# Two quarters of the last inverse step in one two-bank PSUM buffer

## The chip, the core and the metric

The kernel runs on one core of a Trainium2 chip. Its engines each work through a queue of their own in order: TensorE (PE in the profile) multiplies matrices into PSUM, ScalarE (ACT) and VectorE (DVE) read PSUM and write SBUF, GpSimd (POOL) works on SBUF alone, and SyncE (SP) issues nearly all transfers. PSUM has eight banks of 512 fp32 numbers on each of 128 partitions. The metric is the device time of one execution in microseconds (us), lower is better.

## What is computed

A gate per position mixes two branches of the same input `u` (2048 positions, 640 channels): a long convolution (S4D) and a dense layer with ReLU.

```python
K = 2.0 * jnp.einsum("dn,dnl->dl", C, P).real           # kernel of 2048 taps per channel
y = jnp.fft.irfft(rfft(u, 2L) * rfft(K, 2L), 2L)[:L]     # long convolution
a = y + u * D_skip
b = jnp.maximum(x @ w1, 0) @ w2                          # 640 -> 1728 -> 640
g = sigmoid((x * gate_w).sum(-1))
return g * a + (1 - g) * b
```

## The kernel before

The 640 channels of the convolution are done in five tiles of 128 (called tile 0 to tile 4 here, `i` in the code). In each tile the transforms are small matrix multiplications on PE, with their results in PSUM tiles named `pc`, from a pool of three buffers of two banks each (the ring `psc`):

- stage 1 (constants `tf`): the transform along one index of the taps (tiles `ck`, `cl`) and of the input (`xu`); VectorE transposes the results into the tile `ku`.
- stage 2 (`tm`): eight products for a tile, each 16 matmuls into one `pc` buffer. ScalarE copies one bank (`COPY ku<-pc`, 512 columns), VectorE multiplies with the other (two `TENSOR_TENSOR ku<-pc,ku`), GpSimd adds and subtracts. The buffer comes free after the second multiplication.
- inverse step 2 (`tn`): two halves of 64 matmuls, two `pc` buffers each, copied back by ScalarE; then eight transposes on VectorE (`STREAM_TRANSPOSE ku<-ku`), the relays.
- inverse step 1 (`tw`, function `inv1`): the last step. It is cut in four quarters per tile, a pair for each of `j = 0, 1`. A quarter is two matmuls of 512 columns, one for each half of the partitions, that fill one bank. ScalarE then scales it with the gate in four instructions (`ACTIVATE yo<-pc,gate`). Before, each quarter takes a whole `pc` buffer of two banks and leaves the second bank empty.

The dense layer runs beside this. Its 128-wide products write the other two banks (tiles `pf`) and fill PE between the steps of the convolution. It is done in three passes over parts of the hidden width; sums of a pass are loaded (`q<-part`), scaled on ScalarE (`ACTIVATE q<-q,omg`), added to on VectorE (`q<-pf,omg,q`) and stored (`part<-q`, `out_dram<-q`). A `q` load waits for stores of the same rows, and on SP's queue it stands behind other transfers, the loads `yj<-part` among them. Finished convolution rows leave through `yo`: stored to a scratch tensor `y_`, or added to the dense rows and stored to the output.

The order is not written by hand. Every group of instructions is a task with a duration, dependencies, a priority and the ring slots that it takes and uses. `Plan.run` (line 222) simulates the five engines with these numbers when the program is built and calls the tasks in that order; the recorded order of each engine is then kept. A buffer token goes back to its ring when all the tasks that take or use it are through. So a change of who takes a slot changes the order of everything behind it. The planner's rings, and the order that comes from them, set no wait by themselves: the waits that the program holds are derived from the tiles that its instructions read and write.

Of the kernel before, what the change touches and what calls it, by code (L numbers as in the profile page):

```python
# [10 lines left out]
F32 = mybir.dt.float32  # L11
# [14 lines left out]
S4R = 3  # L26
# [318 lines left out]
class Kernel:  # L345
# [865 lines left out]
    def conv(self, C=128):  # L1211
        tc, nc, io, A, tok, ring = self.tc, self.nc, self.io, self.plan.add, self.plan.token, self.plan.ring
# [6 lines left out]
        st = {}  # L1219
# [8 lines left out]
        def table(k, shape, src):  # L1228
            def go():
                st[k] = self.pr.tile(shape, F32, name=k)  # L1230
                D_.dma_start(st[k], io[src])
            return A('SP', 'tab', 0.62, go, [opened], kb=math.prod(shape) * 4 / 1024, rank=3)
# [34 lines left out]
        K, first, pes = {}, {}, {}  # L1267
# [126 lines left out]
        def inv1(i, j, dep):  # L1394
            last = i == n - 1
            for q in range(2):
                b_, b0 = tok('psc'), j * 8 + q * 4
                ns = min(max(2 * sum(c <= i for c in CG) - b0, 0), 4)
                y_ = tok('yo') if ns or not last else None
                g_, first = None, False  # L1400
                if last and ns < 4:
                    first = self.gy_tok is None
                    g_ = self.gy_tok = self.gy_tok or tok('K')

                def pe(q=q, b0=b0):
                    py = st['p4', i, b0] = self.psc.tile([128, 2, 4, C], F32, name="pc")
                    for h in range(2):
                        self.E.matmul(py[h * 64:h * 64 + 64, 0].rearrange("p b c -> p (b c)"), st['tw'],
                                      st['K', i][:, h * 4 + b0 // 4], start=True, stop=True)

                def copy(q=q, b0=b0, ns=ns, y_=y_, first=first):
                    if first:
                        self.gy = self.pr.tile([128, 8, 2, 512], F32, name="ku", bufs=2).rearrange("p j k (b c) -> p (j k b) c", c=C)
                    if y_:
                        st['yo', i, b0] = self.pr.tile([128, 4, C], F32, name="yo", bufs=YO)
                    x = st['p4', i, b0][:, 0].rearrange("p b c -> p (b c)").rearrange("p (c b) -> p b c", b=4)
                    for b in range(4):
                        o = self.gy[:, b0 + b] if last and b >= ns else st['yo', i, b0][:, b]
                        S.mul(o, x[:, b], self.gate[:, b0 + b:b0 + b + 1])
                a = A('PE', 's4', 0.87, pe, [*dep, tw], take=[b_], use=[K[i]], rank=S4R, mode='c1')  # L1420
                pes['4', i, b0] = a
                if JS4 and q:
                    self.plan.join([pes['4', i, b0 - 4], a])
                c = A('ACT', 's4', 1.24, copy, [a], take=[x for x in (y_, g_ if first else None) if x],
                      use=[b_] + ([g_] if g_ and not first else []), rank=S4A)
                self.need_gates.append(c)
                if ns < 4:
                    if not last:
                        def store(b0=b0, ns=ns):
                            stq.dma_start(self.sc['y'][:, b0 + ns:b0 + 4, i * C:i * C + C], st['yo', i, b0][:, ns:])  # L1430
                        c2 = A(STQ, 'y4', 0.62, store, [c], use=[y_], kb=64 * (4 - ns), rank=STR, late=True)
                    self.y_st[i, b0 // 4] = c if last else c2
                if ns:

                    new = not last or b0 == 0
                    if last:
                        j_ = self.yl_tok = tok('cu') if new else self.yl_tok
                    else:
                        j_ = tok('yj')

                    def load(b0=b0, ns=ns):
                        if last:
                            if b0 == 0:
                                st['yl'] = self.xu[:, :16 * C].rearrange(
                                    "p (b c) -> p b c", c=C)
                            st['yj', i, b0] = st['yl'][:, b0:b0 + 4]
                        else:
                            st['yj', i, b0] = self.pr.tile([128, 4, C], F32, name="yj", bufs=YJ)
                        for b in range(0, ns, 2):
                            D_.dma_start(st['yj', i, b0][:, b:b + 2],  # L1450
                                         self.sc['part'][(len(PARTS) - 1) % 2][(b0 + b) // 2][:, :, i * C:i * C + C])

                    def join(b0=b0, ns=ns):
                        y = st['yo', i, b0][:, :ns]
                        P.tensor_add(y, y, st['yj', i, b0][:, :ns])

                    def out(b0=b0, ns=ns):
                        for h in range(2):
                            stq.dma_start(od[h, :, b0:b0 + ns, i * C:i * C + C], st['yo', i, b0][64 * h:64 * h + 64, :ns])
                    ld = A('SP', 'yq', 0.62 * ((ns + 1) // 2), load, [opened], take=[j_] if new else (), use=() if new else [j_],  # L1460
                           kb=64 * ns, rank=3)
                    self.need_sums.append((ld, [(b0 + b) // 2 for b in range(0, ns, 2)]))
                    own = A('POOL', 's4', 0.1 + 0.3 * ns, join, [c, ld], use=[y_, j_], rank=2)
                    A(STQ, 'y4', 1.25, out, [own], use=[y_], kb=64 * ns, rank=STR, late=True)
# [6 lines left out]
        tm, tw, tn = table('tm', [128, 32, 64], 't_m'), table('tw', [128, 64], 't_w'), table('tn', [128, 8, 2, 2, 64], 't_n')  # L1471
        lk.update({q: load_k(0, q) for q in range(2, 4)})
        dep = [x for q in range(4) for x in stage1('k', 0, q, lk[q])]
        dep += [x for q in range(4) for x in stage1('u', 0, q, u)]
        for i in range(n):
            more = i + 1 < n
            if more:
                u = load_u(i + 1)
            fs = [stage2(i, j, [*dep, tm]) for j in range(8)]
            iv = [inv2(i, h, [x for j in range(4 * h, 4 * h + 4) for x in fs[j][1]]) for h in range(2)]  # L1480
            for j in range(8):
                self.plan.put(fs[j][0], 's2')
                if JS2 and j % 2:
                    self.plan.join([fs[j - 1][0], fs[j][0]])
                if j == 3 + LATE:
                    [self.plan.put(x, 's2') for x in iv[0][0]]
            [self.plan.put(x, 's2') for x in iv[1][0]]
            xs, new = [x for _, y in iv for x in y], []
            if more:
                for q in range(4):  # L1490
                    new += stage1('k', i + 1, q, load_k(i + 1, q))
            rl = [relay(i, r, xs) for r in range(8)]
            if more:
                for q in range(4):
                    new += stage1('u', i + 1, q, u)
            for j in range(2):
                inv1(i, j, rl)
            dep = new
# [42 lines left out]
```

## Time and profile before

| | us |
|---|---|
| median of 3 runs | 644.57 (643.60 to 645.45) |
| the profiled execution | 642.35 |
| its span in the profile | 640.6 |

| engine | busy, us | share of the span |
|---|---|---|
| PE (matmul) | 617.3 | 96% |
| DVE | 508.5 | 79% |
| ACT | 402.1 | 63% |
| POOL | 93.9 | 15% |

The convolution's part of the span begins at about 407 us and the first `tw` at 478 us. The granted PE clock is at full speed in every slice. In the timeline a row is a run of equal instructions: start, length, engine, operation, count; in brackets the idle time before it and what ended it. An fp32 matmul (`tf`, `tm`, `tn`, `tw`) leaves two records, so a quarter of `tw` shows as x4 and a product of `tm` as x32; the `pf` matmuls leave one each. Since matmul ends are modelled, a wait of PE is read best from start to start. Nearly all rows carry line 314, that of a helper which records every operation, so one goes by the tiles' names.

### The profile page before, as it was taken

What the parts mean: (1) busy time and instruction counts of PE and PEld (TensorE: products, weight loads), DVE (VectorE), ACT (ScalarE), POOL (GpSimd) and SP (SyncE); (2) the same over time, 40 slices, a digit from 0 to 9 for tenths busy, and PEclk for the clock granted to TensorE, in tenths of its full rate; (3) what the DMA queues carried; (4) which work ended last, traced back from release to release, by engine and by line L of the source; (5) the groups of instructions that cost most, each with busy time, mean ns of one, the idle gap of its engine ahead of it and who ended that gap; (6) DMA issues with size and microseconds to landing.
All of it is one profiled execution on the core that took longest, in us unless ns stands there. A gap on an engine that the chain in (4) does not pass through costs nothing.

```text
span 640.6 us, 19212 instructions
## 1 busy us (share of the span) xinstructions
PE 617.3 (96%) x8236; PEld 503.0 (79%) x8236; DVE 508.5 (79%) x818; ACT 402.1 (63%) x603; POOL 93.9 (15%) x134
## 2 busy tenths in 40 slices
PE   7989999899999899999999999999999999999897
PEld 6989998798898798898898898665565556756577
DVE  4889936989999999998999999768579753966542
ACT  5557439999999988988978985113443424432550
POOL 0000000000000000000000000024151531713633
PEclk9999999999999999999999999999999999999999
DMA  9974774333456734373454225794406558156355
GB/s 256 326 236 147 221 229 165 105 125 112 136 167 210 255 122 144 122 242 117 129 198 154 79 80 176 258 315 132 144 3 215 185 164 263 53 158 188 102 166 133
DMA packets 76176, 107.78 MB, mean 168 GB/s; under 512 B 7610, under 2 KB 58682, under 8 KB 75195
## 3 DMA queue, kind: packets, MB, share of 16 engines
q1 hardware_dynamic: 75930, 106.14, 53.2%
q8 instruction: 65, 1.06, 0.7%
q10 hardware_dynamic: 160, 0.41, 0.3%
q14 instruction: 21, 0.16, 0.1%
HBM read 67.47 MB, written 44.30 MB: 174 GB/s over the span
## 4 chain that ended last, share of the span: by engine, by line
PE 56%; DVE 5%; DMA 2%; ACT 2%; issue 1%; SPq 1%; DVEq 0%; ACTq 0%
PE pf L314 35%; PE pc L314 13%; PE pk L314 4%; DVE ku L314 3%; PE pg L314 2%; PE px L314 2%; DMA part<-q 1%; ACT ku L314 1%; PE pe L314 1%; DMA out_dram<-yo 1%; SPq L314 1%; DVE sn L314 1%; ACT cs L314 0%; DVE q L314 0%; ACT q L314 0%
## 5 line engine op out<-in xcount | busy, mean ns | idle before, releaser
L314 PE MATMUL pf<-xx,w1h 128*128 128x256 f32 (+1 forms) x760 | 184.2, 339 | 0.4 <-DVE xx L314 0.3
L314 PEld LDWEIGHTS pf<-xx,w1h 128*128 128x128 f32 x760 | 125.2, 189 | 22.8 <-issue 7.3
L314 PE MATMUL pf<-xx,w1l 128*128 128x512 f32 (+1 forms) x340 | 115.7, 340 | 0.0
L314 PE MATMUL pf<-w2h,hh 128*128 128x320 f32 x288 | 89.7, 315 | 2.4 <-DVE hl L314 1.5
L314 PE MATMUL pf<-w2l,hh 128*128 128x320 f32 x288 | 87.8, 309 | 0.0
L314 ACT COPY ku<-pc 128x512 f32<-128x512 f32 (+1 forms) x60 | 43.8, 761 | 68.2 <-PE pc L314 56.7
L314 PE MATMUL pf<-w2h,hl 128*128 128x320 f32 x256 | 73.3, 312 | 0.0
L314 PEld LDWEIGHTS pf<-xx,w1l 128*128 128x128 f32 x340 | 64.3, 189 | 7.6 <-DVE w1l L314 0.2
L314 POOL TENSOR_TENSOR kt<-kt,dsk 128x8 f32<-128x8 f32 x20 | 10.3, 515 | 392.7 <-DVE kt L314 377.8
L314 POOL TENSOR_TENSOR ku<-ku 128x256 f32<-128x256 f32 x80 | 56.2, 737 | 55.3 <-DVE ku L314 49.1
L314 DVE TENSOR_TENSOR ku<-pc,ku 128x512 f32<-128x512 f32 x80 | 52.6, 684 | 12.5 <-ACT ku L314 11.3
L314 DVE STREAM_TRANSPOSE ku<-pc 128x512 f32<-128x512 f32 x80 | 50.2, 683 | 13.7 <-PE pc L314 13.7
L314 PEld LDWEIGHTS pf<-w2h,hh 128*128 128x128 f32 x288 | 54.1, 188 | 7.7 <-issue 3.7
L314 DVE TENSOR_TENSOR sn<-pg,cs 128x1024 f32<-128x1024 f32 x40 | 48.7, 1217 | 7.5 <-ACT cs L314 7.5
L314 PEld LDWEIGHTS pf<-w2l,hh 128*128 128x128 f32 x288 | 54.1, 188 | 0.6
L314 ACT ACT_TABLE_LOAD x42 | 53.9, 1283 | 0.7
L314 ACT CAST cs<-pg 128x1024 int32<-128x1024 f32 x40 | 40.3, 1008 | 21.2 <-PE pg L314 21.0
L314 DVE TENSOR_TENSOR mg<-mg,cs 128x1024 f32<-128x1024 f32 x40 | 48.9, 1222 | 1.3
L314 PEld LDWEIGHTS pf<-w2h,hl 128*128 128x128 f32 x256 | 46.4, 188 | 3.5 <-issue 2.9
L314 PE MATMUL pc<-ku,tm 64*32 64x256 f32 x1280 | 42.2, 392 | 3.6 <-DVE ku L314 2.4
L314 ACT ACTIVATE cs<-cs,half_pi 128x1024 f32<-128x1024 f32 x40 | 45.6, 1140 | 0.0
L314 ACT ACTIVATE hh<-pf 128x512 fp32r<-128x512 f32 (+1 forms) x40 | 20.5, 513 | 39.4 <-PE pf L314 39.4
(170 smaller groups left out, 1232.5 us busy)
## 6 DMA issues: line engine op xcount, KB each, us to landing
xx<-xt SPq DMA_DIRECT2D x24, 640.0 KB, 6.8
xt<-xx SPq DMA_DIRECT2D x16, 640.0 KB, 3.9
part<-q SPq DMA_DIRECT2D x16, 640.0 KB, 3.4
q<-part SPq DMA_DIRECT2D x16, 640.0 KB, 5.3
ws<-in_B_w_dram SPq DMA_DIRECT2D x20, 320.0 KB, 5.5
kd<-kt SPq DMA_DIRECT2D x80, 64.0 KB, 1.8
ub<-in_A_u_dram SPq DMA_DIRECT2D x10, 512.0 KB, 4.7
xu<-ub SPq DMA_DIRECT2D x5, 1024.0 KB, 6.2
```

What stands on the lines that cost most here:

```text
L314: self._last = self._tc.keep_in_program_order(f(*a, **k))
```

## The change

The token and the tile are taken once for a pair. The first quarter (`q == 0`) takes the token and makes the tile, and writes bank 0; the second quarter uses the same token and tile and writes bank 1. The copies read the bank of their quarter. The token is free again after the copies of both quarters.

```diff
             for q in range(2):
-                b_, b0 = tok('psc'), j * 8 + q * 4
+                b0 = j * 8 + q * 4
+                b_ = b_ if q else tok('psc')
...
-                def pe(q=q, b0=b0):
-                    py = st['p4', i, b0] = self.psc.tile([128, 2, 4, C], F32, name="pc")
+                def pe(q=q, b0=b0, j=j):
+                    if not q:
+                        st['p4', i, j] = self.psc.tile([128, 2, 4, C], F32, name="pc")
+                    py = st['p4', i, j]
                     for h in range(2):
-                        self.E.matmul(py[h * 64:h * 64 + 64, 0].rearrange("p b c -> p (b c)"), st['tw'],
+                        self.E.matmul(py[h * 64:h * 64 + 64, q].rearrange("p b c -> p (b c)"), st['tw'],
                                       st['K', i][:, h * 4 + b0 // 4], start=True, stop=True)
...
-                    x = st['p4', i, b0][:, 0].rearrange("p b c -> p (b c)").rearrange("p (c b) -> p b c", b=4)
+                    x = st['p4', i, j][:, q].rearrange("p b c -> p (b c)").rearrange("p (c b) -> p b c", b=4)
...
-                a = A('PE', 's4', 0.87, pe, [*dep, tw], take=[b_], use=[K[i]], rank=S4R, mode='c1')
+                a = A('PE', 's4', 0.87, pe, [*dep, tw], take=() if q else [b_], use=[K[i]] + ([b_] if q else []), rank=S4R, mode='c1')
```

No instruction is added or taken away on any engine; PE has 5466 in both programs. What changes is the order from the first `tw` on, on all five engines, and the waits. Three places follow.

PE in tile 1, from the last `cl` product of stage 1 on (`pc` results; `pf` rows are the dense layer), before:

```order
L314 MATMUL pc<-cl,tf 64x512 x4
L314 MATMUL pc<-ku,tw 64x512 x4
L314 MATMUL pc<-ku,tm 32x256 x48
L314 MATMUL pf<-w2l_5336,w2h_6512 128x320
L314 MATMUL pf<-w2h_5335,w2l_6513 128x320
L314 MATMUL pf<-w2h_5272,hh_6024 128x320
```

and now:

```order
L314 MATMUL pc<-cl,tf 64x512 x4
L314 MATMUL pc<-ku,tw 64x512 x6
L314 MATMUL pc<-ku,tm 32x256 x32
L314 MATMUL pc<-ku,tw 64x512 x2
L314 MATMUL pc<-ku,tm 32x256 x32
L314 MATMUL pf<-w2l_5336,w2h_6530 128x320
```

Before, two quarters came first and the other two after all eight `tm` products; now all four come at the front, the last of them between the second and the third product.

PE in tile 3, the same place, with the engines whose semaphores each instruction waits for, before:

```order
L314 MATMUL pc<-ku,tw 64x512 [waits DVE_49,PE_49]
L314 MATMUL pc<-ku,tw 64x512
L314 MATMUL pc<-ku,tw 64x512 [waits DVE_49,PE_49]
L314 MATMUL pc<-ku,tw 64x512
L314 MATMUL pc<-ku,tm 32x256 [waits DVE_49,PE_49]
L314 MATMUL pc<-ku,tm 32x256 x15
L314 MATMUL pc<-ku,tm 32x256 [waits PE_49,Activation_49]
L314 MATMUL pc<-ku,tm 32x256 x15
L314 MATMUL pc<-ku,tm 32x256 [waits PE_49,Activation_49]
L314 MATMUL pc<-ku,tm 32x256 x15
```

and now:

```order
L314 MATMUL pc<-ku,tw 64x512 x3
L314 MATMUL pc<-ku,tw 64x512 [waits DVE_49,PE_49]
L314 MATMUL pc<-ku,tw 64x512
L314 MATMUL pc<-ku,tm 32x256 [waits DVE_49,PE_49]
L314 MATMUL pc<-ku,tm 32x256 x15
L314 MATMUL pc<-ku,tm 32x256 [waits PE_49,Activation_49]
L314 MATMUL pc<-ku,tm 32x256 x15
L314 MATMUL pc<-ku,tw 64x512 [waits Activation_49]
L314 MATMUL pc<-ku,tw 64x512
```

The second `tm` product now waits for ScalarE's copies of both quarters of the first pair, and the second quarter of the second pair waits for ScalarE too: the copy of the first quarter, from the other bank of the same tile, stands ahead of it in the program.

ScalarE from tile 3's first `tm` copies to tile 4's dense activations (`COPY ku<-pc 128x512` are the `tm` copies, `128x4x128x2` those of `tn`, `hh` and `w1h` hold activations of the dense layer), before:

```order
L314 COPY ku<-pc 128x512 x3
L314 ACTIVATE q<-q,omg 128x640
L314 COPY ku<-pc 128x512
L314 ACTIVATE q<-q,omg 128x640
L314 COPY ku<-pc 128x512 x4
L314 ACTIVATE yo<-pc,gate 128x128 x8
L314 COPY ku<-pc 128x4x128x2 x2
L314 ACTIVATE hh_8137<-pf 128x512
L314 COPY ku<-pc 128x4x128x2 x2
L314 ACTIVATE hh_8235<-pf 128x512
L314 ACTIVATE q<-q,omg 128x640
L314 ACTIVATE w1h_8256<-pf 128x512
```

and now:

```order
L314 COPY ku<-pc 128x512 x4
L314 ACTIVATE q<-q,omg 128x640
L314 ACTIVATE yo<-pc,gate 128x128 x4
L314 ACTIVATE q<-q,omg 128x640
L314 COPY ku<-pc 128x512 x4
L314 COPY ku<-pc 128x4x128x2 x2
L314 ACTIVATE hh_8126<-pf 128x512
L314 COPY ku<-pc 128x4x128x2 x2
L314 ACTIVATE hh_8225<-pf 128x512
L314 ACTIVATE q<-q,omg 128x640 x2
L314 ACTIVATE w1h_8251<-pf 128x512
```

The first `q` stands one `tm` copy later, the last quarter's copy stands between the two `q`, and later both `q` stand ahead of `w1h` where one stood behind it.

More of the change, by code (lines that the diff above doesn't have):

```diff
@@ L1403, in inv1, with copy @@
                     g_ = self.gy_tok = self.gy_tok or tok('K')
-                def pe(q=q, b0=b0):
-                    py = st['p4', i, b0] = self.psc.tile([128, 2, 4, C], F32, name="pc")
+                def pe(q=q, b0=b0, j=j):
+                    if not q:
+                        st['p4', i, j] = self.psc.tile([128, 2, 4, C], F32, name="pc")
+                    py = st['p4', i, j]
                     for h in range(2):
-                        self.E.matmul(py[h * 64:h * 64 + 64, 0].rearrange("p b c -> p (b c)"), st['tw'],
+                        self.E.matmul(py[h * 64:h * 64 + 64, q].rearrange("p b c -> p (b c)"), st['tw'],
                                       st['K', i][:, h * 4 + b0 // 4], start=True, stop=True)
-                def copy(q=q, b0=b0, ns=ns, y_=y_, first=first):
+                def copy(q=q, b0=b0, ns=ns, y_=y_, first=first, j=j):
                     if first:
```

## The prediction

> **What bounds the kernel now.** I read the page's first part, then the busy time by stretches of 20 us, then PE's timeline and waits where PE is not full, and last the chain that released it.
>
> ```profile
> span 640.6 us, 19212 instructions
> PE 617.3 (96%) x8236; PEld 503.0 (79%) x8236; DVE 508.5 (79%) x818; ACT 402.1 (63%) x603; POOL 93.9 (15%) x134
> ...
> 560.00:580.00 20.00, 19.86 (x251) 10.70 (x250) 14.70 (x26) 6.31 (x18) 3.56 (x3) 1.00 0.59 179
> 580.00:600.00 20.00, 17.40 (x306) 10.28 (x304) 13.61 (x23) 9.13 (x22) 13.00 (x17) 1.00 0.48 135
> 600.00:620.00 20.00, 19.96 (x328) 16.30 (x327) 7.74 (x14) 8.82 (x15) 3.96 (x6) 1.00 0.57 163
> ```
>
> PE is the bound, at a granted clock of 1.00. The change leaves its work as it is, so the time can move only by what PE waits. Between the first `tw` (478 us) and the end, one stretch has a visible hole, 580 to 600 us with 2.6 us idle: tile 3, where the first of the two `tw` pairs and the `tm` products are. PE's timeline there, and its waits from 560 to 604 us:
>
> ```profile
> 478.47 3.28 PE L314 MATMUL pc<-ku,tw 128*64 128x512 f32 x12
> ...
> 581.32 1.94 PE L314 MATMUL pc<-ku,tw 128*64 128x512 f32 x8
> 583.19 2.98 PE L314 MATMUL pc<-ku,tm 64*32 64x256 f32 x96
> 587.82 0.31 PE L314 MATMUL pf<-w2h,w2h 128*128 128x320 f32 x1
> 588.06 3.01 PE L314 MATMUL pc<-ku,tm 64*32 64x256 f32 x96
> 592.72 0.31 PE L314 MATMUL pf<-w2h,w2h 128*128 128x320 f32 x1
> 594.72 1.15 PE L314 MATMUL pc<-ku,tm 64*32 64x256 f32 x32 [1.70 <-DVE ku L314]
> 596.37 1.16 PE L314 MATMUL pc<-ku,tm 64*32 64x256 f32 x32 [0.50 <-DVE ku L314]
> 597.70 1.08 PE L314 MATMUL pc<-ku,tw 128*64 128x512 f32 x4 [0.17 <-DVE ku L314]
> 599.02 1.08 PE L314 MATMUL pc<-ku,tw 128*64 128x512 f32 x4 [0.24 <-DVE ku L314]
> ...
> PE pc L314 <- DVE ku L314: 2.6, 4, 1.7
> ```
>
> Prices from these rows: a quarter of `tw` is 1.87/2 = 0.93 us of PE (581.32 to 583.19, x8 being two quarters), a `tm` product 2.92/3 = 0.97. From start to start, with 0.2 for the step from `pf` to `pc` (588.06 - 587.82), the four waits are 594.72 - 592.72 - 0.2 = 1.8, then 0.7, 0.2 and 0.4 (each start less the one before, less the group's own 1.0 to 1.15 or 0.93): 3.0 us. The chain of waits says whose they are:
>
> ```profile
> 574.45 0.53 DVE q L314
> ...
> 576.53 6.80 DMA part<-q
> ...
> 587.53 4.29 DMA out_dram<-yo
> 591.83 0.83 ACT q L314
> 592.66 0.48 ACT ku L314
> ...
> 593.16 0.70 DVE ku L314
> ```
>
> A store of dense sums (`part<-q`) lands at 583.33, then SP issues five `yj` loads and the load of `q`; ScalarE waits for it until 591.83 (the profile names the landing of a store issued right behind the load), and behind that waiting instruction stand the `tm` copies, for which VectorE and then PE wait. ScalarE and SP at that place and in the tail:
>
> ```profile
> 480.49 3.22 ACT L314 ACTIVATE yo<-pc,gate 128x128 f32<-128x128 f32 x12
> ...
> 582.50 2.18 ACT L314 ACTIVATE yo<-pc,gate 128x128 f32<-128x128 f32 x8 [11.00 <-issue]
> 586.28 0.59 ACT L314 COPY ku<-pc 128x512 f32<-128x512 f32 x1 [0.33 <-PE pc L314]
> 592.56 0.56 ACT L314 COPY ku<-pc 128x512 f32<-128x512 f32 x1
> 593.03 0.83 ACT L314 ACTIVATE q<-q,omg 128x640 f32<-128x640 f32 x1
> 615.43 0.83 ACT L314 ACTIVATE q<-q,omg 128x640 f32<-128x640 f32 x1 [1.89 <-DVE hl L314]
> 616.17 0.58 ACT L314 ACTIVATE w1h<-pf 128x512 fp32r<-128x512 f32 x1
> ```
>
> ```profile
> 586.94 0.54 SPq L314 DMA_DIRECT2D q<-part  x1
> ...
> 601.20 1.16 SPq L314 DMA_DIRECT2D out_dram<-q  x2
> 609.77 0.60 SPq L314 DMA_DIRECT2D q<-part  x1
> ```
>
> So a quarter's copy is 2.18/2 = 1.09 us of ScalarE, a `tm` copy 0.59, a `q` 0.74 from start to start (591.83 to 592.56), and the `q` load takes 591.83 - 586.94 = 4.9 us from issue.
>
> **The change part by part.** No matmul, copy or transfer is added. *Tiles 0 and 2, all quarters in one run.* Before, three quarters take the three buffers and the third starts late: 3.28 us for x12 where 1.94 + 0.93 = 2.87 is its own price, 0.4 too long, of which I take 0.3 for the wait. Now two buffers hold all four quarters, and the second is asked for 0.93 us later, when the copy that frees it is through. Gain 0.3 in tile 0, 0.3 in tile 2 (that row reads 3.28 as well). The next taps (`cl`) wait for the first pair's eight copies, 2.2 us from 480.5, so until 482.7; PE gets there at about 483.0. Nothing lost.
>
> *Tile 1.* The rows before:
>
> ```profile
> 511.23 1.08 PE L314 MATMUL pc<-ku,tw 128*64 128x512 f32 x4
> 512.62 1.08 PE L314 MATMUL pc<-ku,tw 128*64 128x512 f32 x4 [0.31 <-DVE ku L314]
> ...
> L314 DVE TENSOR_TENSOR ku<-pc,ku x80: 649/690/693, 427.0 to 599.5; 128x512 f32<-128x512 f32 x80
> ```
>
> The wait of 512.62 - 511.23 - 0.93 = 0.45 goes, with the place where it stood. New: the second `tm` waits for the copies of two quarters (2.2 us, begun when the first pair is done) while PE has only a quarter (0.93) and a `tm` (0.97) to do: 0.3. The second pair's buffer is then held until its copies, which stand behind ScalarE's next `q`, so `tm` has two buffers, not three. A product needs 0.59 on ScalarE and 2 x 0.69 on VectorE before its buffer is free; after two products PE comes to the fourth when VectorE has done 1.38 of the 2 x 1.38 that it needs: a further 0.4. From the fifth on, ten to fourteen `pf` (0.15 each, below) stand between two products, which is enough. Tile 1: +0.7 - 0.45 = +0.3. On the other side these two waits may be nothing, if the copies start earlier, or 1.4 each, VectorE's whole price of a product; I stay by the sum, since ScalarE and VectorE are otherwise free there. On SP the next taps' loads (`ck`, `cl`) now stand ahead of the `y_` stores that the last quarter's copy waits for: two issues of some 0.6 us (0.54 to 0.6 below and above), so that copy ends 1.2 us later. Its buffer is next wanted by the last `xu` product, which comes later too, by one `cl` and one `xu` product; I take 0, with up to 1.0 on the other side.
>
> *Tile 3.* PE reaches the first `tm` with one quarter more and ten `pf` less behind it: 583.19 + 0.93 - 1.5 - 0.3 = 582.3. The first pair's matmuls end one quarter and one `tm` group earlier, at 581.5; eight copies at 1.09 per quarter make 583.7, and the second `tm`, ready at 583.3, starts there: +0.4. The second pair's second quarter waits for ScalarE's third quarter copy, 584.8, when PE is at 584.7: +0.1. Ten `pf`, two `tm`, twelve `pf`, one `tm` (1.7 + 1.95 + 1.95 + 0.97, switches within) bring PE to 592.3 at the sixth `tm`. It needs the buffer whose last copy stands behind the first `q`. The `q` load follows VectorE's sums (574.45) by the same transfers in the same order; SP's queue gets the sums' store 0.4 us later, because a sum stands behind one more stage-1 product. So `q` is there at 592.2, runs 0.74, the copy 1.09, and the sixth `tm` starts at 594.1: +1.8. After it no product waits, since both `q` and all quarters are through. Tile 3: 0.4 + 0.1 + 1.8 + 0.2 for two more switches between `pf` and `pc` = 2.5 in place of 3.0: -0.5.
>
> On which waits are needed, the Trainium skill ("PSUM — Partial Sum Buffer", section on PSUM bank collisions) has a rule: guard by bank and quadrant, and read one bank while a matmul fills another. By it the second quarter's wait for the copy of the other bank is not needed, and tile 3 would be 0.1 less. The program orders it all the same; no row of before has that case.
>
> *The tail.* The last pairs stand after the last relays:
>
> ```profile
> 617.39 2.48 DVE L314 STREAM_TRANSPOSE ku<-ku 128x512 f32<-128x512 f32 x4
> 620.01 3.65 PE L314 MATMUL pc<-ku,tw 128*64 128x512 f32 x16
> 623.67 13.12 PE pf L314 x88
> ```
>
> Eight `pf` that stood before the last `tw` stand behind it now: 8 x 13.12/88 = 1.2 us. PE would reach `tw` at 620.01 - 1.2 - 0.3 - 0.3 + 0.3 - 0.5 = 618.0. The relays wait for `w1h` in ScalarE's queue: the `q` load (609.77 before) is issued behind the stores of 601.20, which now follow an earlier sum, by 1.1 us; the two `q` then run at 614.3 and 615.1, `w1h` at 615.8, VectorE's low half until 617.1 and two relays (1.24) until 618.3. PE waits 0.3.
>
> Sum: -0.3 - 0.3 + 0.3 - 0.5 + 0.3 = -0.5 us against a span of 640.6. The profiled execution took 642.35; with the change 641.9. The median of the runs shown is 2.2 higher, 644.57: I predict **644.1**, no change within 0.3% (1.9 us), which is about what a measurement of this kernel can tell from none.
>
> **The rivals.** *Faster: the `q` load is in time.* Four copies now stand ahead of `q`, and PE has products to go on with. If the load lands by 590.4 (1.8 earlier), the sixth `tm` does not wait, and the stores that release the tail's load come earlier by the same: 644.1 - 1.8 = 642.3. For it: the load took 4.9 us among stores. Against it: the five `yj` loads and the store before them keep their order, and the store alone took 6.8.
>
> *Slower: the held buffer.* The last quarter's copy stands between two `q`, so a late load now holds a PSUM buffer too, and with it three products. It decides when the load lands after 594.1, 1.9 us later than I take. An earlier load of the same kind took longer:
>
> ```profile
> 510.82 0.60 SPq L314 DMA_DIRECT2D q<-part  x1
> ...
> 516.39 1.55 ACT L314 ACTIVATE q<-q,omg 128x640 f32<-128x640 f32 x2 [4.44 <-DMA q<-part]
> ```
>
> 5.6 us in place of 4.9; were it to take the 6.8 of the store, and the store to go 0.7 later, PE would wait 2.6 more: 646.7. Against it: DMA is used less then (0.48) than before (0.59).
>
> *Slower: two buffers in tile 1.* If each of the six later products waited 0.4, as the fourth does, tile 1 would lose 2.4 more: 646.5. The `pf` between them speak against it.
>
> **Chances.** My forecast 0.43; the load in time 0.26; the held buffer 0.23; tile 1 short of buffers 0.08. The first lies within 0.3%, the second is faster, the last two are slower: faster 0.26, same 0.43, slower 0.31. The range runs from the faster rival less the two new waits of tile 1 that may be nothing (642.3 - 0.7 = 641.6) to the slower one with a further 1.4 for a product (646.7 + 1.4 = 648.1).
>
> **What would show it.** In tiles 0 and 2 one row of x16 `tw` without a late third quarter; in tile 1 short waits of PE at the second and fourth `tm`, by ScalarE and VectorE; in tile 3 the four waits of 594.72 to 599.02 gone, and one of some 1.8 us at the sixth `tm`, released by ScalarE's quarter copy behind `q`; `tw` of tile 4 near 618.3, with 96 `pf` behind it. I am wrong if the sixth `tm` does not wait, or over 3 us, or if `tm` in tile 1 waits more than twice.

## The result: slower by some 2 us

| comparison | changed, us | before, us | ratio (95% interval) |
|---|---|---|---|
| the first | 646.00 (642.31 to 648.84, 18 runs) | 643.47 (641.66 to 645.45, 18 runs) | 1.0038 (1.0020 to 1.0056) |
| repeated with the experiments | 644.79 (12 runs) | 643.24 (35 runs) | 1.0025 (1.0004 to 1.0046) |
| repeated once more | 644.68 (12 runs) | 643.15 (35 runs) | 1.0013 (0.9990 to 1.0036) |

Over the three, the mean of the 42 runs lies 1.8 us above that of before (standard error 0.3): 2.5, 1.8 and 1.0 in turn. The prediction said 644.1, no change; its range held the result. The medians of e8 and e16 in the table of experiments include one run each in a slow state (998.03 and 649.85 us), which their ratios leave out.

The first part of the page of the changed kernel:

```profile
span 644.5 us, 19197 instructions
PE 618.3 (96%) x8236; PEld 504.3 (78%) x8236; DVE 508.9 (79%) x818; ACT 401.9 (62%) x603; POOL 94.0 (15%) x134
```

The work is the same, so the time is in waits of PE. They are, from 400 us on:

```profile
PE pc L314 <- ACT yo L314: 2.8, 4, 1.8
PE pc L314 <- ACT ku L314: 1.5, 1, 1.5
PE pc L314 <- issue: 1.3, 2, 0.9
PE pf L314 <- issue: 0.9, 1, 0.9
PE pc L314 <- DVE ku L314: 0.6, 3, 0.2
```

ScalarE's quarter copies (`ACT yo`) are new at the top. The 1.5 us by `ACT ku` lies ahead of the first `tw`, where before has 1.0. The span can't be set against that of before as a whole: the first `tw`, ahead of which the order is the same, comes at 480.22 us where it came at 478.47. So I count from the first `tw` on. PE's timeline in tiles 0, 2, 3 and the tail:

```profile
480.22 3.65 PE L314 MATMUL pc<-ku,tw 128*64 128x512 f32 x16
...
566.48 3.65 PE L314 MATMUL pc<-ku,tw 128*64 128x512 f32 x16
...
587.82 1.16 PE L314 MATMUL pc<-ku,tm 64*32 64x256 f32 x32 [0.39 <-ACT yo L314]
588.91 1.08 PE L314 MATMUL pc<-ku,tw 128*64 128x512 f32 x4
...
597.00 2.07 PE L314 MATMUL pc<-ku,tm 64*32 64x256 f32 x64 [0.32 <-ACT yo L314]
...
612.36 0.44 PE L314 MATMUL pc<-ku,tn 32*64 32x128 f32 x5 [0.94 <-issue]
...
621.99 3.65 PE L314 MATMUL pc<-ku,tw 128*64 128x512 f32 x16
```

The sixteen matmul records of a tile's four quarters take 3.59 us from start to start (480.22 to the next product at 483.81; 3.58 in tile 2), where twelve and four took 3.21 + 1.00 (1.01 in tile 2): some 0.6 less in each of tiles 0 and 2. In tile 3 the second `tm` waits 0.4 and the sixth 0.3, by the brackets. And tile 1:

```profile
499.35 2.80 PE L314 MATMUL pc<-ku,tw 128*64 128x512 f32 x12
...
503.56 1.16 PE L314 MATMUL pc<-ku,tm 64*32 64x256 f32 x32 [0.34 <-ACT yo L314]
504.64 1.08 PE L314 MATMUL pc<-ku,tw 128*64 128x512 f32 x4
...
507.00 1.15 PE L314 MATMUL pc<-ku,tm 64*32 64x256 f32 x32 [0.19 <-DVE ku L314]
508.07 0.42 PE L314 MATMUL pf<-w2l,w2h 128*128 128x320 f32 x1
508.33 0.31 PE L314 MATMUL pf<-w2h,w2l 128*128 128x320 f32 x1
...
526.19 1.09 PE L314 MATMUL pc<-xu,tf 64*64 64x512 f32 x8
529.04 1.09 PE L314 MATMUL pc<-xu,tf 64*64 64x512 f32 x8 [1.76 <-ACT yo L314]
```

The last `xu` product waits: 529.04 - 526.19 - 0.89 = 2.0 us (0.89 is half of the 1.77 that two such products took before), the largest wait. In the program it takes the buffer of the second pair, and that one's last copy is late on ScalarE. VectorE's, SP's and ScalarE's timelines show why:

```profile
508.86 0.54 DVE L314 SCALAR_TENSOR_TENSOR q<-pf,omg,q 128x320 f32<-128x320 f32 x1
...
509.43 0.33 SPq L314 DMA_DIRECT2D part<-q  x1
...
516.70 0.60 SPq L314 DMA_DIRECT2D q<-part  x1
...
523.85 1.08 SPq L314 DMA_DIRECT2D cl<-kd  x2
525.03 1.08 SPq L314 DMA_DIRECT2D y__84<-yo  x2
...
523.86 1.55 ACT L314 ACTIVATE q<-q,omg 128x640 f32<-128x640 f32 x2 [6.82 <-DMA q<-part]
...
527.84 1.14 ACT L314 ACTIVATE yo<-pc,gate 128x128 f32<-128x128 f32 x4 [1.41 <-DMA y__84<-yo]
```

The two `pf` matmuls at 508.07 end a dense sum. VectorE adds it to `q`, SP stores it (509.43), loads the next `q` behind that store (516.70), ScalarE multiplies `q` when it has landed (523.86), and behind that stand the copies. The same places before, on PE, VectorE and SP (the `q` load and the multiplication stand in the prediction, 510.82 and 516.39):

```profile
498.12 1.94 PE L314 MATMUL pc<-ku,tw 128*64 128x512 f32 x8
499.98 2.99 PE L314 MATMUL pc<-ku,tm 64*32 64x256 f32 x96
502.90 0.41 PE L314 MATMUL pf<-w2l,w2h 128*128 128x320 f32 x1
503.16 0.31 PE L314 MATMUL pf<-w2h,w2l 128*128 128x320 f32 x1
...
503.50 0.55 DVE L314 SCALAR_TENSOR_TENSOR q<-pf,omg,q 128x320 f32<-128x320 f32 x1 [0.16 <-PE pf L314]
...
504.08 0.33 SPq L314 DMA_DIRECT2D part<-q  x1
```

From the first quarter of tile 1 to these two matmuls it took 502.90 - 498.12 = 4.8 us; it now takes 508.07 - 499.35 = 8.7. Two quarters, one `tm` and two waits have come to stand ahead of 0.3 us of `pf`. Counted from the first `tw`, `q` is multiplied at 43.6 us (523.86 - 480.22) where it was at 37.9.

### The profile page after: what moved, and what is told of

Read it like the earlier page. It is cut to its first block, busy times and chain, and to the rows that moved or that the text cites. A ratio compares the mean times of both kernels' runs of the same rounds, so it can differ in the third digit from the quotient of the medians.

```text
span 644.5 us, 19197 instructions
## 1 busy us (share of the span) xinstructions
PE 618.3 (96%) x8236; PEld 504.3 (78%) x8236; DVE 508.9 (79%) x818; ACT 401.9 (62%) x603; POOL 94.0 (15%) x134
## 4 chain that ended last, share of the span: by engine, by line
PE 67%; DVE 10%; issue 7%; DMA 7%; ACT 6%; SPq 2%; POOL 0%; ACTq 0%; DVEq 0%; POOLq 0%
PE pf L314 45%; PE pc L314 12%; PE pk L314 5%; PE pg L314 2%; DMA q<-part 2%; PE px L314 2%; SPq L314 2%; DVE ku L314 2%; DMA part<-q 2%; DMA xu<-in_A_u_dram 1%; DVE sn L314 1%; DVE G L314 1%; DVE mg L314 1%; PE pe L314 1%; ACT cs L314 1%
## 5 line engine op out<-in xcount | busy, mean ns | idle before, releaser
L314 DVE STREAM_TRANSPOSE ku<-ku 128x512 f32<-128x512 f32 x40 | 25.4, 683 | 25.7 <-ACT ku L314 25.7
```

The lines of the kernel that those rows point to most:

```text
L314: self._last = self._tc.keep_in_program_order(f(*a, **k))
```

## The experiments

All times are medians against runs of before beside them; "q at" is the start of tile 1's `q` multiplication less that of the first `tw`, from the one profiled execution of each kernel. There are 12 runs of each kernel, but 11 of e3 and 5 of e2. The ratio is worked out from the runs, so it is not that of the two medians.

| kernel | us | before, us | ratio (95% interval) | q at, us |
|---|---|---|---|---|
| e1 shared, old order | 642.08 | 642.78 | 0.9998 (0.9977 to 1.0019) | 39.4 |
| e2 two more yo | 650.10 | 642.78 | 1.0114 (1.0086 to 1.0143) | 42.1 |
| e3 tiles 0, 2, 4 | 642.52 | 642.78 | 0.9986 (0.9963 to 1.0009) | 35.0 |
| e4 tiles 1, 3 | 643.57 | 642.78 | 1.0020 (0.9998 to 1.0042) | 37.5 |
| e5 copies first | 644.84 | 643.24 | 1.0026 (1.0005 to 1.0047) | 43.4 |
| e6 the change again | 644.79 | 643.24 | 1.0025 (1.0004 to 1.0046) | 42.1 |
| e7 all but tile 1 | 643.04 | 643.24 | 1.0001 (0.9976 to 1.0025) | 35.5 |
| e8 seven yo, planned | 645.00 | 643.24 | 1.0024 (1.0000 to 1.0049) | 37.1 |
| e9 sum first | 643.58 | 643.29 | 1.0015 (0.9990 to 1.0040) | 37.4 |
| e10 before, sum late | 645.08 | 643.29 | 1.0024 (1.0002 to 1.0045) | 42.7 |
| e11 sum and copies first | 643.67 | 643.29 | 1.0012 (0.9992 to 1.0032) | 38.9 |
| e12 sum first, seven yo | 644.18 | 643.29 | 1.0007 (0.9983 to 1.0031) | 35.6 |
| e13 the change once more | 644.68 | 643.15 | 1.0013 (0.9990 to 1.0036) | 42.3 |
| e14 sum first again | 644.21 | 643.15 | 1.0019 (1.0000 to 1.0038) | 36.9 |
| e15 before, sum first | 643.16 | 643.15 | 1.0005 (0.9987 to 1.0024) | 34.4 |
| e16 tiles 0, 2, 4 again | 642.26 | 643.15 | 0.9985 (0.9962 to 1.0007) | 35.7 |
| e17 sum and w1h first | 642.96 | 643.14 | 1.0007 (0.9989 to 1.0025) | 36.9 |
| e18 w1h first alone | 643.66 | 643.14 | 1.0011 (0.9991 to 1.0031) | 43.2 |

**Is it the buffer, the order, or one tile?** My first theory was the held buffer: the second pair's buffer, held in tile 1 until the `q` load has landed. Rivals: the shared tile itself, and the new order as such.

e1 keeps the shared tiles, but the planner still takes a token for each quarter, and each engine's order is that of before:

```diff
-                b_ = b_ if q else tok('psc')
+                b_ = tok('psc')
...
-                a = A('PE', 's4', 0.87, pe, [*dep, tw], take=() if q else [b_], use=[K[i]] + ([b_] if q else []), rank=S4R, mode='c1')
+                a = A('PE', 's4', 0.87, pe, [*dep, tw], take=[b_], use=[K[i]], rank=S4R, mode='c1')
```

> The quarters of a pair share a two-bank tile as in the change, but the planner is told what it was told before (a slot for each quarter), so that all engines keep the order of before. Held buffer (the loss is that in tile 1 the second pair's copies, behind a q load and a y_ store, keep a buffer from the stage-1 products): a pair holds one buffer in place of two, so no loss, 0 to -1.0 us against before. Rival, sharing itself (PE fills one bank while ScalarE reads the other of the same tile): slower by about the 2.5 us of the change. Rival, order (the new order puts instruction-fetch stalls elsewhere): 0.

It is as fast as before, within its interval: two quarters in the two banks of one tile show no cost. So what costs comes with the new order. e2 gives the physical pool two more `yo` buffers (`bufs=YO + 2`), which the planner does not know of, so the order is that of the change:

> The changed kernel, its order kept, with seven yo buffers in SBUF in place of five, so that tile 1's last quarter copy no longer waits for the y_ store. Held buffer: in the changed kernel's profile that wait ends at 527.84 us where ScalarE was free at 526.4, so 1.4 us of the 2.0 us wait at the third xu product goes: 1.1 us slower than before in place of 2.5. Sharing itself and order: 2.5 us slower, as the change.

It came out 7.3 us slower, against every theory. Its row of the same product:

```profile
525.93 3.36 PE L314 MATMUL pc<-xu,tf 64*64 64x512 f32 x16 [4.14 <-ACT yo L314]
```

No copy waits for a `yo` store now, and the pool hands the held buffer to the first `xu` product instead of the last, which asks for it some 5 us earlier (at 521.8 in place of 527.1): 4.1 us of wait in place of 1.8. So how long PE waits for the held buffer depends on which product happens to get it. This explains some 2 us of the 4.8 between e2 and the change (7.3 less the 2.5 of the first comparison). The five runs also had a lower granted clock, 0.991 to 0.995, where those of before had 0.998 in the mean; why, and how much of the rest that is, stays open.

e3 and e4 share in the even and in the odd tiles alone (`pair = i in (0, 2, 4)` and `pair = i in (1, 3)`, the token and the bank following `pair`); e7 shares in all but tile 1 (`pair = i != 1`), and e16 repeats e3:

> Pairs share only in tiles 0, 2 and 4; tiles 1 and 3 take a buffer for each quarter, as before, and the planner orders that anew. Held buffer: the gain of 0.6 us in each of tiles 0 and 2 without the wait in tile 1: faster than before by 0.5 to 1.3 us. Sharing itself: slower by 1 to 1.5 us. Order: anything between, by where the fetch stalls of 0.9 us fall.

> Pairs share only in tiles 1 and 3. Held buffer: the wait at the third xu product of tile 1 is there, and no gain in tiles 0 and 2: slower than before by 2 to 3.5 us, less what tile 3 saves (up to 1.8). Sharing itself: slower by about 1 us.

> Pairs share a buffer in tiles 0, 2, 3 and 4; in tile 1 each quarter has its own, and the planner orders anew. Held buffer in tile 1: tile 1 loses nothing, tiles 0 and 2 gain 0.64 each and tile 3 up to 1.8, so -1.5 to 0 us against before. Rival, that the new order of tile 3 and the tail costs (the odd tiles alone came out 0.7 us above before with no long xu wait in tile 1): +0.5 to +2.

> Pairs share a buffer in tiles 0, 2 and 4 alone, as before: the order that it gets in tile 1 has the sum early. Late sum: -0.2 to -1.0 us against before, from the 0.64 us that tiles 0 and 2 gain each. Rival, no gain from tiles 0 and 2 because it is lost again to later waits: -0.2 to +0.3.

Without tile 1 the change shows no cost; the even tiles alone come out at 0.9986 and 0.9985, which is no more than their intervals. In these kernels the order of tile 1 is close to that of before, with two `pf` right behind the first two quarters, and `q` comes at 35 to 36 us. Of e4 I had expected more: the planner, with separate buffers in tile 0, orders tile 1 as before, so its trace has only 0.6 us of that wait (and 2.8 us in tile 2, behind another `q` load).

**The wait taken away, and nothing gained.** e5 takes the copies out from behind `q`. Both copies are called ahead of the first `q` multiplication, and `yo` has eight buffers:

```diff
+            if (e, t.q) == ('ACT', 'mx') and heads['ACT', 's4'] == 6:
+                for c in self.queues['ACT', 's4'][6:8]:
+                    c.fn()
+                    c.fn = lambda: None
             t.fn()
...
```

> The changed kernel, but in tile 1 the last pair's two copies (of eight yo instructions) stand ahead of the two q multiplications on ScalarE, and yo has eight buffers so that these copies wait for no store. The order of PE is that of the changed kernel. Held buffer (the last pair's one buffer is held until the q load has landed, and the xu product that gets it waits 1.8 to 2.0 us): that wait is gone, so +0 to +1.0 us against before in place of the changed kernel's +2.5. Order and instruction fetch (the +2.5 comes from the longer rows elsewhere): +2 to +3 as with the change.

> The changed kernel again, on the same chip as the three beside it. Both theories: +2 to +3 us against before, with the fourth xu product of tile 1 waiting 1.5 to 2.5 us. If the q load lands earlier in this execution the held buffer says a shorter wait there, and a time that is shorter by as much.

The `xu` wait is gone from its trace, and the time is that of the change, which stands beside it as e6 (both 1.8 us above before in the mean). PE's and ScalarE's rows in tile 2 show a wait of the same size there:

```profile
544.35 2.22 PE L318 MATMUL pc<-ku,tm 64*32 64x256 f32 x64 [1.99 <-ACT ku L318]
...
541.81 1.55 ACT L318 ACTIVATE q<-q,omg 128x640 f32<-128x640 f32 x2 [4.80 <-DMA y__84<-yo]
```

The next `q` is multiplied 541.81 - 478.50 = 63.3 us after the first `tw`, as late as in the changed kernel (543.78 - 480.22 = 63.6), and the copies that tile 2's `tm` needs stand behind it. So the held buffer as the cause fell: it is one place at which a late load becomes visible, and in this trace, without it, the next place takes over. Whether tile 2's `q` is late because of tile 1 isn't shown: in e6 and e13, with the changed order, it comes at 61.9, in that of before at 60.4 and in e1 at 61.8. e8, where the planner knows of seven `yo` buffers (`YO = 7`) and itself puts the copies ahead of `q`, gained nothing either; its trace waits 0.8 and 0.5 us, by the brackets, at two `tm` of tile 2:

> The changed kernel with seven yo buffers in place of five, which the planner knows of: it now places the last pair's copies of tile 1 ahead of q, between the tm copies, and orders later work anew. Held buffer: no xu product waits behind q, so -1 to +0.5 us against before. Order and instruction fetch: +2 to +3.

**The late sum.** The second theory: the loads are late because the sum that they follow is late. e9 and e14 call the two `pf` matmuls ahead of tile 1's first quarter, and the add ahead of the first `tm` multiplication; all else is in the changed kernel's order:

```diff
+            early = None
+            if (e, t.q) == ('PE', 's4') and heads['PE', 's4'] == 4:
+                early = 'PE', 'ff'
+            if (e, t.q) == ('DVE', 's2') and heads['PE', 's4'] in (7, 8) and not getattr(self, 'sum_done', 0):
+                early, self.sum_done = ('DVE', 'ff'), 1
+            if early:
+                c = self.queues[early][heads[early]]
+                c.fn()
+                c.fn = lambda: None
             t.fn()
```

> The changed kernel, but in tile 1 the two last matmuls of a dense sum (pf) stand ahead of the first quarter of tw, and VectorE's add of that sum (q) ahead of the first tm multiplication; all else in the changed kernel's order. Late sum (in the changed order these two matmuls of 0.15 us each stand behind two more quarters, one more tm and two new waits, so that the sum's store, and the q load behind it, start 3.9 us later, and the held buffer and tile 2's copies wait for loads): the q load lands some 7 us earlier than with the change, no xu product waits, and the time is 0 to +0.7 us against before in place of +1.6 to +2.5. Rival, the new order itself and instruction fetch: +1.5 to +2.5 as with the change.

> The changed kernel with the two pf matmuls and their add first in tile 1, as before, now beside the changed kernel on one chip. Late sum: 0 to +0.7 us against before. Rival: +1.5 to +2.5.

> The changed kernel, on one chip with the sum-first kernels beside it. Late sum: +1.5 to +2.5 us against before, and 1 to 2 us above the changed kernel with the sum first. Rival, the order itself: +1.5 to +2.5, and within 0.5 us of the changed kernel with the sum first.

e10 does the reverse to the kernel before: no buffer is shared, but the same two matmuls, the add and the store are held back until after the sixth `tm`:

```diff
...
+            if held and getattr(self, 'products', 0) >= 3 and (e, t.q) == ('PE', 'ff'):
+                for c in held:
+                    c.fn()
...
+            if ((e, t.q) == ('PE', 'ff') and heads['PE', 's4'] == 6 and not hasattr(self, 'products') and not held
+                    or any(d in held for d in t.deps)):
+                held.append(t)
+            else:
+                t.fn()
```

> The kernel before, no buffer shared, but in tile 1 the same two pf matmuls, the add and the store of their sum stand behind the fourth to sixth tm product in place of the third. Late sum: the store goes some 5.4 us later, the q load and the quarters' copies behind it too, an xu product waits 2 to 4 us, and the time is +1.5 to +3.5 us against before without any change of buffers. Rival, the shared buffer and its order: -0.3 to +0.5.

> The kernel before with the same two matmuls and their add ahead of tile 1's first quarter; its sum then goes some 2.4 us earlier than before. Late sum: before, the quarters' copies behind q come just in time, so an earlier sum gains little, -0.7 to 0 us. If the sum's time counts in proportion (1.8 us lost for 5.4 later): -0.8.

The late sum alone, without any change of buffers, makes the kernel before 1.8 us slower (medians; 1.4 in the mean, standard error 0.6). Its `q` comes at 42.7 us, as in the changed kernel, and an `xu` product waits, though only 0.65 us:

```profile
523.54 1.55 ACT L326 ACTIVATE q<-q,omg 128x640 f32<-128x640 f32 x2 [8.96 <-DMA out_dram<-yo]
...
526.17 1.09 PE L326 MATMUL pc<-xu,tf 64*64 64x512 f32 x8 [0.65 <-ACT yo L326]
...
546.79 0.48 PE L326 MATMUL pc<-ku,tn 32*64 32x128 f32 x16 [1.83 <-issue]
```

So the place of the sum sets when `q` lands: it is at 42 us or later in every kernel with the late sum (the change three times, e2, e5, e10, e18) and at 34 to 39 in all others. That this makes the time is less sure: 1.8 us in this trace are a stall at 546.79 that the profile puts down to no one, and e8 is as slow with `q` at 37.1. An earlier sum in the kernel before (e15) gains nothing, as expected: there the copies were in time.

In the changed kernel the early sum does what it should in the trace. Of e14, ScalarE and PE:

```profile
516.38 1.55 ACT L323 ACTIVATE q<-q,omg 128x640 f32<-128x640 f32 x2
...
525.64 1.95 PE L323 MATMUL pc<-xu,tf 64*64 64x512 f32 x16
...
618.88 3.65 PE L323 MATMUL pc<-ku,tw 128*64 128x512 f32 x16 [1.73 <-DVE ku L323]
```

`q` stands at 516.38 - 479.47 = 36.9 us after the first `tw`, and the two last `xu` products run without a wait. But the time did not follow clearly: 0.3 us above before is left in e9 and 1.1 in e14, and e13, the change beside e14 on the same chip, is no slower than e14 by more than the noise: 644.68 against 644.21 us in the median, 644.50 against 644.56 in the mean. That is what e13's rival, the order itself, had asked for. e11 and e12, which add the two edits of `yo` to the early sum, lie in the same range:

> Both edits on the changed kernel: the sum first, and the last pair's copies of tile 1 ahead of q with eight yo buffers. Late sum: the copies no longer matter, so the same as the sum first alone within 0.5 us, 0 to +0.7 against before. If the held buffer costs by itself too: 0.5 to 1.5 us less than the sum first alone.

> The changed kernel with seven yo buffers that the planner knows of (+1.5 us before) and the sum first in tile 1. Late sum: -0.5 to +0.5 us against before. Rival, the new order itself: +1 to +2.

**The second place.** The last row above shows another wait: PE now waits 1.73 us at the very last `tw`. ScalarE's and VectorE's rows of e14 there:

```profile
614.77 1.55 ACT L323 ACTIVATE q<-q,omg 128x640 f32<-128x640 f32 x2 [3.79 <-DMA q<-part]
616.23 0.57 ACT L323 ACTIVATE w1h<-pf 128x512 fp32r<-128x512 f32 x1
...
616.84 0.69 DVE L323 SCALAR_TENSOR_TENSOR w1l<-pf,w1h 128x512 fp32r<-128x512 f32 x1 [2.71 <-ACT w1h L323]
617.44 1.29 DVE L323 STREAM_TRANSPOSE ku<-ku 128x512 f32<-128x512 f32 x2
```

In the changed order both `q` stand ahead of `w1h`, `w1l` waits for that, and the last two relays, for which the `tw` waits, stand behind `w1l` on VectorE. The changed kernel has that wait too in two of its three traces, 1.15 us in e6 and 1.17 in e13, and e9 has 2.54; in the first trace PE comes too late for it. Of e13, PE in tile 1 and in the tail:

```profile
527.38 1.09 PE L314 MATMUL pc<-xu,tf 64*64 64x512 f32 x8 [1.40 <-ACT yo L314]
...
618.77 3.65 PE L314 MATMUL pc<-ku,tw 128*64 128x512 f32 x16 [1.17 <-DVE ku L314]
```

e18 puts `w1h` ahead of the last two `q` in the changed kernel (the two and what depends on them are held until ScalarE's next dense task has been called), e17 does so together with the early sum:

```diff
...
+            if ((e, t.q) == ('ACT', 'mx') and heads['ACT', 'mx'] >= len(self.queues['ACT', 'mx']) - 2
+                    or any(d in held for d in t.deps)):
+                held.append(t)
+            else:
+                t.fn()
+                if held and (e, t.q) == ('ACT', 'ff'):
+                    for c in held:
+                        c.fn()
+                    held.clear()
```

> The changed kernel with the sum first in tile 1, and in the tail ScalarE's w1h ahead of the last two q in place of behind them (before, one of the two stood behind it). Two places in a row (the late sum, then the relays of tile 4, which wait for w1h behind both q, so that PE waits 1.3 to 1.9 us at the last tw as soon as it gets there earlier): the last tw waits under 0.5 us, and the time is -1.5 to -0.2 us against before. Rival, another wait takes this place too: +0.5 to +1.2, as with the sum first alone.

> The changed kernel with w1h ahead of the last two q alone, the sum in tile 1 left late. Two places in a row: PE comes to the last tw late, so only the 0.1 to 1.3 us that it waited there in the changed kernel's traces goes, +0.5 to +1.5 us against before. If the tail alone makes the change slower: -0.5 to +0.3.

With both, neither wait is left. The tail of e17:

```profile
618.09 0.60 ACT L332 ACTIVATE w1h<-pf 128x512 fp32r<-128x512 f32 x1 [2.81 <-PE pf L332]
618.59 1.54 ACT L332 ACTIVATE q<-q,omg 128x640 f32<-128x640 f32 x2
...
619.33 1.30 DVE L332 STREAM_TRANSPOSE ku<-ku 128x512 f32<-128x512 f32 x2
...
621.39 3.65 PE L332 MATMUL pc<-ku,tw 128*64 128x512 f32 x16
```

From the first `tw` to the start of the last sixteen it takes 621.39 - 483.06 = 138.3 us, where the changed kernel took 621.99 - 480.22 = 141.8, e6 140.8, e13 139.9, e18 140.3 and e14 139.4; e9, profiled at a granted clock of 0.947, took 142.5. With the order of before e1 took 139.5, of which 1.2 are eight `pf` that the changed order puts behind: the same as e17. The time of e17 is that of before (642.96 against 643.14). In means against before: the change +1.8 us (42 runs, standard error 0.3), the sum first +1.0 (24 runs, 0.5), `w1h` first +0.5 (12 runs, 0.6), both +0.4 (12 runs, 0.5). With both edits the time can't be told from before, and the two waits are gone from the trace. That these two waits are the loss is argued, not shown: e18 is as fast as e17 in the mean, though its trace keeps the `xu` wait and waits 0.85 us more at the sixth `tm` of tile 3:

```profile
527.67 1.09 PE L323 MATMUL pc<-xu,tf 64*64 64x512 f32 x8 [1.75 <-ACT yo L323]
```

How the loss divides isn't settled either: one wait hides part of the other, and the single edits differ by no more than their errors.

A rival is left, which the expectations name: PE's stalls that the profile lists under "issue", put elsewhere by the new order. From the first `tw` on they sum to 2.3, 1.5 and 0.7 us in the three traces of the change, and to 0.3 in that of before and none in e1's. Against it, they sum to 2.4 in e7, 2.0 in e16 and 1.2 in e15, which are no slower than before. No run here separates them from the waits, and none shows that they come from instruction fetch. No version here beats before by more than its interval; the even tiles alone come nearest.

## Why the prediction was wrong

- *Tiles 0 and 2:* right in kind, the late third quarter is gone; some 0.6 us each in place of 0.3. The term took only the wait, not the two groups becoming one.
- *Tile 1, the two `tm` waits:* right. Predicted 0.3 and 0.4; two `tm` in a row take 2.57 us from start to start (502.07 to 504.64) and 2.42 (505.65 to 508.07) where 2.00 is normal, so 0.6 and 0.4, at the second and fourth `tm`, by ScalarE and VectorE.
- *Tile 1, the last quarter's copy:* this is the step that failed. The prediction put the copy 1.2 us later, for two issues on SP, and took 0 for the `xu` product, with up to 1.0 on the other side. It never asked when `q` itself lands in tile 1. The sum ahead of it goes 3.9 us later, `q` is multiplied 5.7 us later, and the product waits 2.0 us in the first trace, 1.4 and 1.6 in e6 and e13 (1.2 and 1.4 by their brackets). The wait is shown; that the time grows by it is not, since e5 takes it away and is no faster. The prediction knew the mechanism: it gave tile 3's sum 0.4 for "one more stage-1 product", and its rival of the held buffer describes exactly this wait, with a price of 2.6. It looked for it in tile 3, where the trace of before had a hole, and not in tile 1, where PE's packed run of quarters and `tm` leaves the two `pf` behind.
- *Tile 3:* predicted 2.5 in place of 3.0, with 1.8 at the sixth `tm`. In the first trace it is 1.1 in place of 3.0 (0.6 at the second and 0.5 at the sixth, from start to start), and in e6 and e13 the sixth does not wait at all, which the prediction named as a sign of being wrong. But the 3.0 itself was in that one execution of before. With the same order e1 has, in the same place,

```profile
594.60 2.11 PE L314 MATMUL pc<-ku,tm 64*32 64x256 f32 x64
596.88 1.94 PE L314 MATMUL pc<-ku,tw 128*64 128x512 f32 x8 [0.17 <-DVE ku L314]
```

 and e10 the row

```profile
599.05 2.06 PE L326 MATMUL pc<-ku,tm 64*32 64x256 f32 x64
```

 without the 1.70 and 0.50 of before; e15, with its sum early, has no such hole either. By start to start what is left in e1 and e15 is 0.8 and 0.9. A gain against a hole that these three traces don't have can hardly show in a median.
- *The tail:* predicted 0.3 of wait for relays behind `w1h` behind two `q`. The mechanism is right, the size was not: 0.1 in the first trace, where PE comes late, 1.2 in e6 and e13, 1.7 in e14 and 2.5 in e9.
- *The sum, mended:* -1.3 for tiles 0 and 2, +1.0 for the `tm` waits less the 0.45 gone, +1.4 to 2.0 for the `xu` product, nothing for tile 3 (0.6 to 1.1 against e1's 0.8), +0.1 to 1.2 in the tail: +1.4 in the first trace, 1.8 in e6 and 2.1 in e13, against a measured 1.8. The size fits, but "issue" stalls are not in this sum, and the single edits did not change the time as its terms say.
- *What was luck:* set against the profiled execution of before, hole and all, the first trace has -1.3 + 1.0 - 0.45 + 2.0 + 1.1 - 3.0 + 0.1 = some -0.6 us of waits, close to the predicted -0.5. That is chance: 0 was taken where 2.0 came, and 2.5 where 1.1 came. Between these two traces it is the "issue" stalls, 2.3 us against 0.3, that make the changed kernel longer up to the last `tw`: -0.6 + 2.0 = 1.4, and 141.77 - 141.54 + 1.2 for the eight `pf` put behind = 1.4.
- *The second quarter of a pair:* the prediction weighed the Trainium skill's rule ("PSUM — Partial Sum Buffer", section on PSUM bank collisions), by which the second quarter's wait for the copy of the other bank isn't needed. Here it made no time: the quarter at 588.91 starts 1.09 us after the `tm` at 587.82, with no idle time ahead of it, and e1 shows no cost of the shared tile.

## What to carry to other kernels

When products are packed closer, look for the last small instruction of another chain that now stands behind them: here 0.3 us of matmul ended a sum, and a store, a load of 5 to 7 us and an in-order ScalarE hung on it. When several waits hang on one stream of loads, taking away the first can uncover the next, as in the traces of e5 and e14, so an experiment that removes one wait must be read at the next two places as well, not by its time alone. And a hole in one profiled execution is worth a forecast only if other executions of the same order have it.

## What was not expected of the hardware

- A transfer that has nothing to do with `q` waited for its load. The chain of waits and SP's timeline of the changed kernel:

```profile
516.70 7.08 DMA q<-part
...
520.81 1.33 SPq L314 DMA_DIRECT2D ck<-kd  x2
```

 The `q` load lands at 523.78. SP's issue before it ends at 522.14, yet the `cl` load is issued only at 523.85, right behind that landing. SP's waits put this, 1.6 us, down to the `q` load, the eighth transfer before it, though by the tiles' names the two share no data. In e2 the same issue comes at 522.26, behind a landing at 522.21. So here a late load also stopped SP's queue, eight transfers on, and the `y_` store that the last copy needs stood behind it. What ties the two transfers together isn't shown.
- PE's stalls that the profile lists under "issue" move from trace to trace: 0.94 and 0.94 in the changed kernel (539.33 and 612.36), 1.39 in e2 (548.64), 1.83 in e10 (546.79), 0.3 in all in that of before. They are as large as the terms of the prediction's sum, and what they are stays open.
- The runs of one kernel follow the granted clock, though not by a fixed rate. Of the 157 runs of before beside the experiments, the 56 at 0.999 and above took 642.3 us in the mean and the 21 at 0.995 and below 645.8; but one run of e9 at 0.947 took no more than 647.3. Such a spread is larger than what was to be measured, so a difference of 2 us shows only in the mean of many runs.
